# Replacing a list planner by a written-out time for every piece of work

## The chip, the cores and the metric

The kernel runs on one core of one Trainium2 chip. A core has five engines with a queue of instructions each: TensorE (PE), VectorE (DVE), ScalarE (ACT), GpSimd (POOL) and SyncE (SP). Each works through its own list in order, and a semaphore holds an instruction until work of another engine is done. The time is device microseconds (us) of one launch; lower is better.

## The reference, cut to what matters

`x` is 2048 tokens by 512. Four layers follow one another, A, B, A, B, each added to `x` after a layer norm.

```
# A: attention over segments of 32 tokens, 8 memory rows carried from segment to segment
mem = mem0
for s in range(64):
    h = concatenate([mem, x[32*s : 32*s+32]])            # 40 rows
    q, k, v = h@Wq, h@Wk, h@Wv                           # 32 heads of 128
    p = softmax(mask(q @ k.T * scale))                   # mask: the memory columns are open
    o = (p @ v) @ Wo
    mem = o[:8];  outs.append(o[8:])                     # the next segment needs mem

# B: linear attention, 32 heads of 16
q, k, v = split(x @ wqkv);  phi = where(t > 0, t+1, exp(t)) + 1e-6
kv = phi(k).T @ v;  z = sum(phi(k))                      # over all 2048 tokens
o = (phi(q) @ kv) / (phi(q) @ z) @ wo
```

So an A layer is a recurrence of 64 steps that can't be split: the memory rows of step s+1 come out of the whole of step s. A B layer needs sums over all tokens before its second half can begin.

## The kernel before, in words

All weights lie in SBUF. `a_layer` is called twice, and each call walks 64 steps; four steps make a tile of 128 tokens. A step consists of these pieces (names as in the code, with the profile's lines):

- `k0`, `k1`, `q0`, `q1`, `v0`, `v1`: `project`, six PSUM tiles of four nodes each. A node is four matmuls side by side, each on 32 columns of the array, 512 wide (L811 for q and k, L815 for v). Each tile is copied to SBUF by ACT or DVE (L625 or L626; `evac` lets the planner choose), and for q and k DVE turns it with a STREAM_TRANSPOSE (L834).
- `mem0`, `mem1`: attention of the 8 memory rows, for two halves of the heads: scores (L916, L910), exp on ACT (L927), two products on DVE (L937), sums on PE (L751), log and exp on ACT (L947, L949), values on PE (L751), a product on DVE (L960).
- `out`: eight nodes of eight 256-wide matmuls (L1056), the first four reading the first half of the heads, then two copies into `outW_sb`.
- `next`: two small PE nodes (L1081) and one copy, which give the memory rows of the next step. The chain k, q, mem, out, next is the recurrence.
- `x`: attention of the 32 token rows, whose result is only needed by the `out` of the following step (L978, L992, L988, L995, L997, L999, L1000, four copies `Pbx` of 32x256, L1011, PE L751).
- `res`: rows of the result go through `y_sb` (L1092) and by small DMAs of POOL (L641) into `dx_sb`, and are added to `x`.

Every fourth step has more: `prep` (layer norm of the next tile and its transposition, L776), `left0`, `left1`, `leftv0`, `leftv1`, `lefts` (q, k, v of the last 8 rows of the tile's four segments, six tiles more of `project`), the rows of `out` that belong to them (`left_rows`), `bi` (`b_in`: first half of B for a finished tile), and in the second A layer `bo` (`b_out`: second half of B for a tile of the layer before).

Nothing is emitted in the order of the code. `_Prog.add` records a node with its reads, writes and PSUM tiles; `_Prog.schedule` is a list planner. It keeps a clock for every engine, gives each node a duration from formulas (`c_act`, `c_dve`, `c_pe4`), and hands each engine the ready node of highest priority:

```
nd.prio = -(step * PERIOD + OFFSET[name][k])             # PERIOD = 13.5, OFFSET a table of 600 numbers by name
spare = 0 if tiles[oldest[0]] in nd.tiles else 1 if nd.urgent else 2
if bf is None or bf[1] > tn + EPS or n_free(tn + EPS) <= spare:
    kept.append(item)                                    # no PSUM bank for it: wait
```

A first writer of a PSUM tile takes one of eight banks, and a tile that is not `urgent` (not on the recurrence) has to leave two banks free and to wait until all other inputs of its later nodes are done (`soft`). All nodes of one tile are chained in the order of the code: each waits for the one before.

Two helpers add matmuls that compute nothing that is used: `warm` (14 of 512 in the first step, L742) and `keep_busy` (151 of 256, L1352), the latter around the ends of both A layers.

`_Prog.finalize` turns dependences into semaphore waits, and `emit` writes each engine's list.

## Time and profile before

| | |
|---|---|
| median of 3 runs | 1823.23 us (1821.59 to 1824.45) |
| profiled execution: its own time | 1821.27 us |
| profiled execution: span from first to last instruction | 1819.1 us, mean granted clock 0.995 |
| PE busy | 1626.0 us, 89% of the span, 53422 matmuls |
| DVE busy | 1175.7 us, 65% |
| ACT busy | 1137.4 us, 63% |
| POOL busy | 327.1 us, 18% |

A matmul's recorded duration holds its way through the array, so PE can be counted busy while no matmul is being fed. "Idle before" a group is time in which the engine stood still just before one of its instructions, with the work that ended the wait behind the arrow. `PEclk` is the share of full speed that PE's clock was granted. The chain that ended last is followed back from the last instruction.

In the trace the first layer A runs from the first `k` of step 1 at 53.48 us to the `out` of step 64 (the token rows of the last segment) at 878.92 us, the second from 925.48 us to 1780.00 us.

### The profile page before, as it was taken

The numbers are of one execution on the slowest core, as the hardware profiler recorded it, in microseconds if no ns is written. First come the engines' busy times: TensorE is split into PE (matmuls) and PEld (weight loads), VectorE is DVE, ScalarE is ACT, GpSimd is POOL, SyncE is SP. The second block draws the span as 40 slices with busy tenths as digits, with TensorE's granted clock in tenths as the row PEclk, the third lists the DMA queues.
The fourth block names the chain that finished last, engine by engine and source line by source line (L and its number), as shares of the span: only waits on it lengthen the run. The fifth ranks groups of instructions, "written<-read, shape, count | busy, mean of one in ns | idle before, by whom it ended". The sixth has DMA issues, their size and how long they took to land.

```text
span 1819.1 us, 115216 instructions
## 1 busy us (share of the span) xinstructions
PE 1626.0 (89%) x53422; PEld 1044.7 (57%) x53422; DVE 1175.7 (65%) x3945; ACT 1137.4 (63%) x3132; POOL 327.1 (18%) x660
## 2 busy tenths in 40 slices
PE   5899888999998999899989989999889999889898
PEld 2556555655555565555655555555555565555564
DVE  3566666666666666666566766666666666666667
ACT  3566666666666666666466666666666666666655
POOL 2012121111212111112101221121211121211121
PEclk9999999999999999999999999999999999999999
DMA  9100000000000000000000000000000000000004
GB/s 377 54 15 13 16 16 12 12 15 16 13 15 16 12 13 15 16 15 19 16 8 12 19 15 16 18 18 12 18 15 15 18 16 15 18 13 17 24 13 142
DMA packets 34929, 51.66 MB, mean 28 GB/s; under 512 B 13432, under 2 KB 28592, under 8 KB 32912
## 3 DMA queue, kind: packets, MB, share of 16 engines
q0 software_dynamic: 21744, 19.78, 3.8%
q1 hardware_dynamic: 11120, 11.94, 2.0%
q10 hardware_dynamic: 1584, 12.58, 1.7%
q8 instruction: 417, 6.83, 1.5%
q14 instruction: 64, 0.52, 0.1%
HBM read 29.63 MB, written 10.49 MB: 22 GB/s over the span
## 4 chain that ended last, share of the span: by engine, by line
PE 72%; DVE 12%; ACT 10%; DMA 3%; issue 3%; POOL 0%; DVEq 0%; ACTq 0%
PE pb L811 31%; PE pb L815 13%; PE pb L1056 12%; PE pb L751 10%; DVE arena_sb L626 5%; ACT arena_sb L625 4%; DVE arena_sb L960 2%; ACT outW_sb L625 2%; PE pb L910 2%; DMA Wk_sb<-in_A_Wk_dram 1%; DVE arena_sb L999 1%; PE pb L776 1%; ACT arena_sb L949 1%; PE pb L1081 1%; ACT arena_sb L927 1%
## 5 line engine op out<-in xcount | busy, mean ns | idle before, releaser
L625 ACT ACTIVATE arena_sb<-pb 128x512 bf16<-128x512 f32 (+6 forms) x1423 | 696.5, 502 | 357.9 <-PE pb L811 198.7
L834 DVE STREAM_TRANSPOSE arena_sb<-arena_sb 128x256 f32<-128x256 f32 x640 | 278.7, 440 | 269.7 <-ACT arena_sb L625 268.7
L641 POOL DMA_DIRECT2D dx_sb<-y_sb x504 | 254.4, 511 | 1056.6 <-DVE y_sb L1092 565.9
L1056 PE MATMUL pb<-Wo_sb,arena_sb 128*32 128x256 bf16 x10368 | 349.3, 274 | 58.9 <-DVE arena_sb L960 55.2
L751 PE MATMUL pb<-arena_sb 128*32 128x128 bf16 (+2 forms) x14320 | 333.2, 223 | 46.5 <-DVE arena_sb L626 23.8
L811 PE MATMUL pb<-Wk_sb,arena_sb 128*32 128x512 bf16 x5120 | 337.6, 383 | 37.9 <-ACT arena_sb L625 16.5
L815 PE MATMUL pb<-Wv_sb,arena_sb 128*32 128x512 bf16 x5120 | 348.3, 378 | 0.5 <-issue 0.4
L811 PE MATMUL pb<-Wq_sb,arena_sb 128*32 128x512 bf16 x5120 | 341.9, 382 | 0.7 <-DMA Wq_sb<-in_A_Wq_dram 0.6
L1056 PEld LDWEIGHTS pb<-Wo_sb,arena_sb 128*32 128x32 bf16 x10368 | 256.2, 97 | 107.1 <-DVE arena_sb L960 81.5
L751 PEld LDWEIGHTS pb<-arena_sb 128*32 128x32 bf16 x14320 | 232.5, 96 | 137.0 <-DVE arena_sb L626 47.8
L626 DVE CAST arena_sb<-pb 128x128 bf16<-128x128 f32 (+3 forms) x351 | 162.7, 470 | 104.0 <-PE pb L815 55.1
L811 PEld LDWEIGHTS pb<-Wk_sb,arena_sb 128*32 128x32 bf16 x5120 | 127.2, 97 | 159.1 <-ACT arena_sb L625 27.2
L811 PEld LDWEIGHTS pb<-Wq_sb,arena_sb 128*32 128x32 bf16 x5120 | 137.1, 97 | 125.0 <-issue 4.0
L625 ACT ACTIVATE outW_sb<-pb 128x128 fp32r<-128x128 f32 x247 | 68.5, 277 | 161.8 <-PE pb L1056 154.1
L626 DVE COPY arena_sb<-arena_sb 32x256 bf16<-32x256 bf16 (+1 forms) x615 | 130.9, 213 | 46.1 <-PE pb L910 26.2
L815 PEld LDWEIGHTS pb<-Wv_sb,arena_sb 128*32 128x32 bf16 x5120 | 123.9, 95 | 64.0 <-issue 2.1
L927 ACT ACTIVATE arena_sb<-pb 128x192 bf16<-128x192 f32 (+1 forms) x256 | 84.1, 328 | 59.5 <-PE pb L910 57.5
L960 DVE TENSOR_TENSOR arena_sb<-pb,arena_sb 128x128 bf16<-128x128 f32 x252 | 71.7, 287 | 70.0 <-PE pb L751 37.9
L937 DVE TENSOR_TENSOR arena_sb<-arena_sb 128x128 bf16<-128x128 bf16 x504 | 88.5, 216 | 9.2 <-ACT arena_sb L927 7.2
L1092 DVE TENSOR_TENSOR y_sb<-pb,outW_sb 64x256 bf16<-64x256 f32 x158 | 65.8, 416 | 27.1 <-ACT outW_sb L625 23.5
L751 PE MATMUL pb<-arena_sb,one_sb 128*32 128x128 bf16 x2016 | 71.9, 220 | 10.1 <-DVE arena_sb L937 10.1
L751 PEld LDWEIGHTS pb<-arena_sb,one_sb 128*32 128x32 bf16 x2016 | 48.8, 96 | 47.8 <-DVE arena_sb L937 27.6
(103 smaller groups left out, 1524.1 us busy)
## 6 DMA issues: line engine op xcount, KB each, us to landing
Wq_sb<-in_A_Wq_dram ACTq DMA_DIRECT2D x1, 4096.0 KB, 13.8
Wk_sb<-in_A_Wk_dram ACTq DMA_DIRECT2D x1, 4096.0 KB, 24.5
Wv_sb<-in_A_Wv_dram ACTq DMA_DIRECT2D x1, 4096.0 KB, 34.9
Wo_sb<-in_A_Wo_dram SPq DMA_DIRECT2D x4, 1024.0 KB, 11.8
xs_scratch<-x_sb POOLq DMA_DIRECT2D x32, 128.0 KB, 2.3
pq_scratch<-arena_sb POOLq DMA_DIRECT2D x32, 128.0 KB, 2.0
dx_sb<-y_sb POOLq DMA_DIRECT2D x252, 12.0 KB, 1.7
dx_sb<-y_sb POOLq DMA_DIRECT2D x252, 4.0 KB, 1.8
```

What stands on the lines that cost most here:

```text
L625: return e.activation(o() if callable(o) else o, i() if callable(i) else i, ACTF.Copy)
L626: return e.tensor_copy(o() if callable(o) else o, i() if callable(i) else i)
L641: add(eng, lambda e: e.dma_start(o, i), 0.55 if eng == "pool" else 0.4, reads=reads, writes=writes, dsem="%s%d" % (kind, k), lat=lat + (0. ...
L751: r = pe.matmul(o[q], w[:, q], x, start=start, stop=stop, skip_group_check=True, tile_position=(0, 32 * j))
L811: r = pe.matmul(tl.f32()[32 * j:32 * j + 32, 0:512].rearrange("p (i j f) -> p i j f", i=4, j=4), blk[:, c, :], w, start=(c == 0), stop=(c ...
L815: r = pe.matmul(tl.f32()[32 * j:32 * j + 32, 0:512], blk[:, c, :], W[:, c, o:o + 512], start=(c == 0), stop=(c == 3), tile_position=(0, 32 ...
L834: add("dve", lambda v: v.transpose(dst, src(img[:, k, :].bitcast(F32))), c_dve(256), reads=[("img", k)], writes=[dkey], urgent=urgent)
L927: add("act", lambda a: a.activation(PQ[:, r2, b, 0:nq], tl.f32()[:, 0:nq], ACTF.Exp, scale=SCALE), c_act(nq), tiles=[tl], writes=[("PQ", r ...
L937: add("dve", lambda v, a=a, p_=p_, w_=w_: v.tensor_tensor(wide(Pm[:, k, a, :]), p_.unsqueeze(2).to_broadcast([128, 4, 4, 8]), w_, ALU.mult ...
L960: add("dve", lambda v: v.tensor_tensor(oTb[:, s % NO, 16 * b:16 * b + 16, 0:8], pv.f32()[:, 0:128].rearrange("p (n q) -> p n q", q=8), Rm[ ...
L1056: r = pe.matmul(tl.f32()[32 * j:32 * j + 32, 0:256], oT[:, 4 * hh + n, :], Wo_sb[:, 8 * n + hh, 256 * d:256 * d + 256], start=(hh == 0 and ...
L1092: add("dve", lambda v: v.tensor_tensor(y_sb[0:64, k, :], tl.f32()[0:64, 0:256], outW[64:128, w, :].bitcast(F32), ALU.add), c_dve(256), rea ...
```

## The change

The planner goes. Each node carries a written time, in ns, and often a letter for its engine (a for ACT, v for DVE). For each layer `PERIOD` holds a length of four steps, an offset, and a table by name and step modulo four; `OWN` has entries for single steps, mainly near both ends of each layer, which come before the table.

```
PERIOD = {
    0: (44811, 8548, {
        'k0': {
            0: '27075 27835 28266 28482 28937a 29591',
...
        'next': {
            0: '37244 37304 37674a',
            1: '48363 48423 48793a',
...
    1: (47082, 762505, {
...
OWN = {
    (0, 0, 'next'): '49733 49894 50264v',
...
def when(key, engs):
    layer, step, name, k = key
    own = _OWN.get((layer, step, name), ())
    if k < len(own) and own[k] is not None:
        t, eng = own[k]
    else:
        n, o, table = _PERIOD[layer]
        t, eng = table[name][step % 4][k]
        t += o + n * (step // 4)
    return t, eng or engs[0]
```

The times are used for one thing: the order. `schedule` becomes a sort, a walk that hands out banks (the one whose last reader stands earliest), and a pass over the readers of each tile:

```
for nd in self.nodes:
    nd.t, nd.eng = when(nd.key, nd.engs)
seq = sorted(self.nodes, key=lambda n: (n.t, n.idx))
...
        b = min(free)[1]
        if owner[b] is not None:
            for o in owner[b].ops:
                (nd.order if o.eng == "pe" and nd.eng == "pe" else nd.sync).add(o)
...
for tl in {tl for nd in seq for tl in nd.tiles}:
    ops = sorted(tl.ops, key=lambda o: place[o])
    for i, nd in enumerate(ops):
        if nd.eng != "pe":
            for o in ops[:i]:
                if o.eng not in ("pe", nd.eng):
                    nd.sync.add(o)
self.committed = seq
```

In `add` a reader of a tile now waits for the last matmul of the tile rather than for the reader that stands before it in the code; readers on different engines wait for one another in the order of their times, readers on one engine need no wait. Further:

```
-    def warm(step, n, after):
...
-    def keep_busy():
...
-    keep_busy()
+    P.before["act"] = add("act", lambda a: a.preload_act_table_set("natural_log_exp_and_others"), 1.3)
-                add("pe", mm, c_pe4(4, 512), reads=[key] + bkeys, tiles=[tl], urgent=urgent, mode="col")
+                add("pe", mm, 0.2155, reads=[key] + bkeys, tiles=[tl])
```

The last pair stands for many such edits of a node's duration. `urgent`, `soft`, the spare banks, `mode` and the fence are gone. The nodes that compute something are the same.

How the order comes out can be read without a run, from the two built programs. The four-step pattern of PE in the middle of the first layer, from the `out` of one step to the projections of the next (line numbers of the changed file: L1560 is `out`, L1584 `next`, L1318 q and k, L1322 v; in brackets what an instruction waits for):

```
L1560 Matmult pb<-Wo_sb,arena_sb 32x256 [s_act,s_dve]
L1560 Matmult pb<-Wo_sb,arena_sb 32x256 x31
L1318 Matmult pb<-Wq_sb,arena_sb 32x512 x4
L1318 Matmult pb<-Wk_sb,arena_sb 32x512 x4
L1318 Matmult pb<-Wq_sb,arena_sb 32x512 x4
L1584 Matmult pb<-selm_sb,outW_sb 32x16 [s_dve]
L1584 Matmult pb<-selm_sb,outW_sb 32x16 x3
L1322 Matmult pb<-Wv_sb,arena_sb 32x512 [s_act]
L1322 Matmult pb<-Wv_sb,arena_sb 32x512 x3
L1584 Matmult pb<-selm_sb,outW_sb 32x16 [s_act]
L1584 Matmult pb<-selm_sb,outW_sb 32x16 x3
L1318 Matmult pb<-Wq_sb,arena_sb 32x512 x4
L1318 Matmult pb<-Wk_sb,arena_sb 32x512 x4
L1318 Matmult pb<-Wq_sb,arena_sb 32x512 x4
L1318 Matmult pb<-Wk_sb,arena_sb 32x512 [s_act]
L1318 Matmult pb<-Wk_sb,arena_sb 32x512 x11
```

Before, the same place in the program reads:

```
L1056 Matmult pb<-Wo_sb,arena_sb 32x256 [s_dve]
L1056 Matmult pb<-Wo_sb,arena_sb 32x256 x31
L751 Matmult pb<-arena_sb 32x128 [s_dve]
L751 Matmult pb<-arena_sb 32x128 x11
L751 Matmult pb<-arena_sb 32x128 [s_dve]
L751 Matmult pb<-arena_sb 32x128 x3
L751 Matmult pb<-arena_sb 32x16x8 x4
L1081 Matmult pb<-selm_sb,outW_sb 32x16 [s_act]
L1081 Matmult pb<-selm_sb,outW_sb 32x16 x3
L751 Matmult pb<-arena_sb 32x128 x12
L751 Matmult pb<-arena_sb 32x128 [s_dve]
L751 Matmult pb<-arena_sb 32x128 x3
L751 Matmult pb<-arena_sb 32x16x8 x4
L1081 Matmult pb<-selm_sb,outW_sb 32x16 [s_act]
L1081 Matmult pb<-selm_sb,outW_sb 32x16 x3
L811 Matmult pb<-Wk_sb,arena_sb 32x512 [s_dve]
L811 Matmult pb<-Wk_sb,arena_sb 32x512 x19
```

Counted over the whole program: 165 matmuls fewer on PE (the helpers'); matmuls that carry a wait 2140 before and 2483 after, waits that stand alone on PE 56 and 322. Of the copies, 158 of 32x256 and 54 of 128x128 in SBUF go from DVE to ACT, 43 of the `outW_sb` copies too; 102 of 128x512 out of PSUM and 37 of 128x384 go from ACT to DVE. SP's eight loads of the last stage, four before of one array and then four of the other, are mixed (two, one, two, three).

## The prediction

> **What bounds the kernel now.** I read the page first: busy shares, the clock, the chain that ended last; then PE's waits; then PE's timeline over four steps.

> ```profile
> PE 1626.0 (89%) x53422; PEld 1044.7 (57%) x53422; DVE 1175.7 (65%) x3945; ACT 1137.4 (63%) x3132; POOL 327.1 (18%) x660
> PEclk9999999999999999999999999999999999999999
> PE 72%; DVE 12%; ACT 10%; DMA 3%; issue 3%; POOL 0%; DVEq 0%; ACTq 0%
> ```

> PE leads, at full clock, yet 22% of the chain lies on DVE and ACT: PE isn't saturated, it stands in a ring with them. Whom it waits for (total, times, longest):

> ```profile
> PE pb L1056 <- DVE arena_sb L960: 55.2, 104, 1.0
> PE pb L751 <- DVE arena_sb L626: 23.8, 60, 2.6
> PE pb L811 <- ACT arena_sb L625: 16.5, 46, 0.6
> PE pb L811 <- DVE arena_sb L626: 15.8, 39, 0.7
> PE pb L751 <- issue: 4.0, 6, 1.7
> ```

> All are links of the recurrence: `out` waits for the memory product, the next projections for the copy after `next`. In one step of the timeline (start, duration, idle before):

> ```profile
> 656.97 1.26 PE L811 MATMUL pb<-Wk_sb,arena_sb 128*32 128x512 bf16 x20 [0.34 <-DVE arena_sb L626]
> 658.06 1.04 PE L811 MATMUL pb<-Wq_sb,arena_sb 128*32 128x512 bf16 x16
> 658.92 0.82 PE L811 MATMUL pb<-Wk_sb,arena_sb 128*32 128x512 bf16 x12
> ...
> 662.30 0.39 PE L815 MATMUL pb<-Wv_sb,arena_sb 128*32 128x512 bf16 x4
> 663.07 0.29 PE L751 MATMUL pb<-arena_sb,one_sb 128*32 128x128 bf16 x8 [0.38 <-DVE arena_sb L937]
> ...
> 664.55 1.93 PE L1056 MATMUL pb<-Wo_sb,arena_sb 128*32 128x256 bf16 x64 [0.40 <-DVE arena_sb L960]
> 666.70 0.46 PE L751 MATMUL pb<-arena_sb 128*32 128x128 bf16 x20 [0.22 <-DVE arena_sb L626]
> ...
> 667.92 1.26 PE L811 MATMUL pb<-Wk_sb,arena_sb 128*32 128x512 bf16 x20 [0.37 <-DVE arena_sb L626]
> ```

> Two things are to be seen. Where work is at hand PE is fed without a hole: 16 matmuls in 658.92-658.06=0.86 us, 53.9 ns each. And each step has five holes; a hole is longer than "idle before" says, since the last matmul's way through the array (1.93 us for 64, of which 64x27.2 ns=1.74 is feeding) counts as busy.

> **What PE must do.** Feeding times by such differences: 53.9 ns (512 wide), 27.2 (256), 13.9 (128), some 7 (32 to 64). In four steps: 480 of k, q, v, left and 32 of `b_in` at 512 wide, 27.6 us; 320 of `out`, 8.7; 368 at 128 wide, 5.1; 16 of L992, 0.4; some 400 small ones, 2.8. Sum **44.6 us, 11.15 a step**. `b_out` adds 16 at 512 and 16 at 128 in layer two: 45.7, 11.43 a step. Before takes (878.92-53.48)/63=13.10 and (1780.00-925.48)/63=13.56. So 1.95 and 2.13 us a step are holes: 123+134=257 us. More can't be won in the steps.

> **The change part by part.**

> *The order.* I compare PE work standing between a producer and its consumer in the new order (front part, and the same period's other rows) with the traced chain between them.
> - `out` to `next`: drain 0.17, copy into `outW_sb` 0.28, two hand-overs of 0.03 to 0.05: 0.52 us. New cover: 12 matmuls of 512, 0.65; in the other three step kinds 0.65 to 0.79. Before: 0.22 idle here after 0.2 of drain.
> - `next` to k: drain 0.17, copy 0.20, hand-overs 0.08: 0.45. Cover 0.58 to 0.65, by `left` and values of the token rows. Before: 0.34 to 0.39 idle.
> - Scores to sums: drain 0.17, exp 0.33, two products 0.36, hand-overs 0.12: 0.98. Cover: 16 of L1322, 24 of 128 wide, the other half's scores: 1.3. Before: 0.38 idle.
> - Sums to `out`: drain 0.17, L947 0.28, L949 0.31, L960 0.29, hand-overs 0.15: 1.20. Cover 1.5 to 1.7. Before: 0.40.

> Every hole has cover, by 0.1 to 0.5 us. The cover holds only if ACT or DVE isn't busy with something else when its turn comes. *Engine letters*: ACT gains 158x411 (32x256 copies) +54x309+43x277 and loses 102x597+37x489 ns, with small ones +19 us; DVE loses 158x219+54x192+43x289 and gains 102x689+37x554, +29 us. That is 1156 and 1205 us, 73% and 76% of some 1590: both below PE (1471 us of feeding, 92%), but fuller than now, so queues form. From none to half of the holes can stay. I take 0.28 us a step: 0.08 is the trace's own `issue` pauses (some 10 us, no order removes them), 0.20 about one thin cover missed per step. Nearest row: from 688.31 to 707.62 us, where `left` gave PE enough to do, the timeline shows no idle at all; that speaks for the low end.

> *Waits on PE*: 266 more that stand alone. Nearest row: L992, which waits for ACT and DVE, starts at 701.53, just 8x53.9 ns after 701.10 when L815 began. Price 0; upper end 0.05 each, 13 us. *Readers in time order, no waits between readers on one engine, banks by earliest release*: these are in the order; alone they could cost a bank wait or save one hand-over (0.05 us) per tile; 0, both ends inside the holes above. *Durations in `add`*: nothing reads them now; 0. *POOL's and SP's order*: row DMAs land in 1.7 to 1.8 us and are needed many us later except at the ends; the last stage's eight loads still start together after step 63's `out`; 0, -2 to +3.

> *The helpers.* They fed PE 151x107 ns+3.0=19 us, in holes of the layer ends; on the path they cost next to nothing (at 895.24 they end 0.17 after the work they delay), so removal gains under 1 us. What they bought is the clock:

> ```profile
> 24.00:27.00 3.00, 1.23 (x12) 0.46 (x16) 0.00 (x0) 0.00 (x0) 0.00 (x0) 0.50 1.03 429
> 894.00:897.00 3.00, 3.00 (x36) 1.97 (x34) 1.39 (x3) 0.35 (x1) 0.54 (x1) 1.00 0.23 76
> 912.00:915.00 3.00, 1.71 (x92) 1.03 (x92) 2.80 (x12) 2.89 (x9) 0.00 (x0) 0.92 0.15 44
> 915.00:918.00 3.00, 2.78 (x68) 1.63 (x68) 2.67 (x12) 2.19 (x10) 0.00 (x0) 0.51 0.00 0
> ```

> (stretch, length, PE busy, then the other engines; third from the end PEclk.) With helpers the serial part at 894 keeps 1.00; after PE's pause at 21.2 to 25.8, and again after a half-idle stretch at 912, it is halved for some 3 us. [...]

> **The sum**, on the profiled execution's span: head to step 1, 52.5 (53.48 before; bound by the weight DMAs, the last q/k/v one landing after 34.9). Layer one 63x(11.15+0.28)=720. Between the layers, 46.6 before: the serial chain from `out` at 878.92 to the first `left` at 899.85 stays, 20.9; +3 for the clock; then step 0, 25.6 before with a DMA wait of 2.76 on its chain, now some 15 (its PE work is near 14): 39. Layer two 63x(11.43+0.28)=738. Tail, 39.1 before: ACT's Ln and Exp of 16 tiles bound it in any order; less 1 for order, +3 for the clock: 41. Sum 1590.5. The profiled run is 2.2 longer than its span, and the median 2.0 above it: **1595 us**, 12.5% less.

> **The rivals.**
> 1. *The plan holds to the letter*: no hole stays, PE feeds always. 1595-126x0.28=1560. For: every cover is positive. Against: margins of 0.1 us with ACT and DVE at 75%. 15%.
> 2. *Half the holes return as queueing on ACT and DVE*, whose order can't adapt: 1.0 us a step instead of 0.28 is +92: 1687. For: 32x256 copies of 0.41 on ACT may stand ahead of the copy on the chain. Against: the dense stretch above. 20%.
> 3. *Slower*: head-of-line blocking. In the new list a 32x256 copy that waits for DVE (L999 of the token rows) stands ahead of ACT's copies of q and k; if the token chain (exp, sums, log, exp, two products) is late by d, the recurrence is late by d in every step. It decides from d=2.1 us a step beyond its cover (228/126=1.81 on top of the 0.28): all that the order wins. The token chain's pieces sum to some 3 us and it has most of a step. 4%.
> 4. *Nothing changes*: the recurrence's latency, not idle order, sets 13 us. Against: its pieces (k and q 3.5, drain to scores 1.9, mem 2.7, `out` 1.8, `next` 1.5) give 11.4 even in a row, and halves overlap. 1%.

> My forecast, between 1 and 2, 60%. The range 1555 to 1668 takes 1, the clock's and waits' upper ends and some of 2. Faster by over 0.2% (about what a measurement of this kernel can tell) 95%, within it 1%, slower 4%.

> **What would show it.** Right: `out <- L960`, `L811 <- copies` each under a third of now; k to k some 11.4 and 11.7 us; PE busy near all of each mid-kernel slice; DVE and ACT at 73 to 76%; PEclk of 0.5 to 0.8 at the layers' ends and nowhere else. Wrong: PE waits on ACT's copies of q and k of half a us each (case 2), or POOL's row DMAs on the chain in mid-layer, or a lower clock in the steps.

## The result, and the profile after

The kernel with the written order takes **1699.62 us** (median of 4, 1698.46 to 1702.65) against 1823.84 for the kernel before, measured beside it (4 runs, 1821.59 to 1824.46): a ratio of **0.9324, 95% interval 0.9307 to 0.934**. It is faster, as forecast, but 105 us slower than the forecast 1595, and 32 us outside the range. The profiled execution took 1702.65 us, its span 1700.9.

From the profile, in the same order as before the change (busy shares, PE's clock, the chain that ended last):

```profile
PE 1555.4 (91%) x53257; PEld 1096.2 (64%) x53257; DVE 1170.0 (69%) x3811; ACT 1133.5 (67%) x3266; POOL 325.7 (19%) x660
PEclk9999999999999999999899999999999999999998
PE 82%; DVE 6%; issue 6%; ACT 4%; DMA 2%; POOL 0%; DVEq 0%; ACTq 0%
```

DVE's and ACT's share of the chain fell from 22% to 10%. But `issue` doubled from 3% to 6%: time in which PE waited for nothing that the profile shows. PE's waits (total us, times, longest):

```profile
PE pb L1560 <- issue: 26.0, 35, 3.8
PE pb L1261 <- issue: 25.0, 36, 1.4
PE pb L1318 <- DMA Wq_sb<-in_A_Wq_dram: 20.1, 1, 20.1
...
PE pb L1318 <- ACT arena_sb L1150: 5.2, 16, 0.4
...
PE pb L1560 <- DVE arena_sb L1466: 0.2, 1, 0.2
```

L1560 is `out`, L1466 the memory product ahead of it: 55.2 us of waiting became 0.2. So the order did what it was to do. In its place stand `issue`, some 70 us over all lines (about 10 before), and one wait of 20 us for Wq at the start.

By stage, with the same marks as in the prediction:

| stage | forecast | after | excess |
|---|---|---|---|
| head, to the first projection of step 1 | 52.5 | 61.08 | 8.6 |
| layer one, 63 steps | 11.43 each | (827.46-61.08)/63=12.17 | 0.74 each, 46 |
| between the layers | 39 | 867.29-827.46=39.8 | 0.8 |
| layer two, 63 steps | 11.71 each | (1657.32-867.29)/63=12.54 | 0.83 each, 52 |
| tail | 41 | 43.6 | 2.6 |

The sum of the excess is the 110 us by which the span missed 1590.5. Nine tenths of it lie in the steps. PE's timeline in one step shows what kind of pause it is (start, duration, form, number of matmuls, idle before):

```profile
640.95 1.55 PE L1560 MATMUL pb<-Wo_sb,arena_sb 128*32 128x256 bf16 x48
643.23 0.40 PE L1560 MATMUL pb<-Wo_sb,arena_sb 128*32 128x256 bf16 x6 [0.73 <-issue]
643.36 0.89 PE L1261 MATMUL pb<-arena_sb 128*32 128x128 bf16 x46
644.03 0.21 PE L1584 MATMUL pb<-selm_sb,outW_sb 128*32 128x16 f32 x4
644.08 0.23 PE L1261 MATMUL pb<-arena_sb 128*32 128x128 bf16 x2
644.13 0.29 PE L1584 MATMUL pb<-selm_sb,outW_sb 128*32 128x16 f32 x12
644.25 0.29 PE L1498 MATMUL pb<-arena_sb,bo_sb 128*32 128x256 bf16 x4
644.36 0.21 PE L1494 MATMUL pb<-arena_sb,bo_sb 128*32 128x64 bf16 x4
644.39 0.63 PE L1261 MATMUL pb<-arena_sb 128*32 128x128 bf16 x32
644.84 0.83 PE L1318 MATMUL pb<-Wk_sb,arena_sb 128*32 128x512 bf16 x12
645.48 0.40 PE L1318 MATMUL pb<-Wq_sb,arena_sb 128*32 128x512 bf16 x4
645.70 0.39 PE L1318 MATMUL pb<-Wk_sb,arena_sb 128*32 128x512 bf16 x2
646.98 0.39 PE L1318 MATMUL pb<-Wk_sb,arena_sb 128*32 128x512 bf16 x2 [0.90 <-issue]
```

Both pauses stand in the middle of a node: after 58 of the 64 matmuls of `out`, and after two of a node's four. No semaphore is waited for there. From one pause to the next there are 6+46+4+2+12+4+4+32+12+4+2=**128 matmuls**. With a weight load each that is 256 instructions. The DMA table has a queue that carries PE's instructions (packets, MB, share of the 16 engines):

```profile
q8 instruction: 417, 6.83, 1.7%
```

6.83 MB in 417 packets is 16,384 bytes each, and PE's 2x53257 instructions and 322 stand-alone waits, divided by 256, make 417.3; out512 (below), with 5184 matmuls and as many weight loads fewer, has 377 packets in this queue. I call the 256 instructions of such a packet a page. The 128 matmuls above were fed in 645.70+2x0.054-643.23=2.58 us, and the next page was there 3.75 us after the first.

Setting the trace's packets of q8 beside PE's starts (worked out from the trace): 194 of the 417 pages begin with a pause, 115 us in all (start to start of the two matmuls, less 40 ns). The pause stands ahead of instruction 192 of each 256 (within 2), counted from PE's first. So do all 107 of the profile's `issue` waits of PE (70.5 us), and all 16 (10.3 us) of the kernel before. PE resumes 1.26 to 1.56 us after a packet's end (10th to 90th percentile). In the median a packet starts 1.1 us after PE enters a page and takes 1.03 us; a page that ends in a pause has then lasted 3.5 us. 99 of 100 packets start at least 3.3 us after the one before. At 416 of the 417 places where PE enters a page, the packets that had ended were just as many as the pages entered before it. So here only one page was fetched ahead, and over several pages PE got no more than 128 matmuls in some 3.3 to 3.5 us (a single page can be shorter, down to 2.4 us, where the one before it was long). In the two layers the pauses come to 0.90 and 0.86 us a step. By the same count the kernel before has 36 of them, 18 us.

### The profile page after: what moved, and what is told of

Same layout as the page of the kernel before. It is cut to its first block, busy times and chain, and to the rows that moved or that the text cites. A ratio compares the mean times of both kernels' runs of the same rounds, so it can differ in the third digit from the quotient of the medians.

```text
span 1700.9 us, 115242 instructions
## 1 busy us (share of the span) xinstructions
PE 1555.4 (91%) x53257; PEld 1096.2 (64%) x53257; DVE 1170.0 (69%) x3811; ACT 1133.5 (67%) x3266; POOL 325.7 (19%) x660
## 3 DMA queue, kind: packets, MB, share of 16 engines
q8 instruction: 417, 6.83, 1.7%
## 4 chain that ended last, share of the span: by engine, by line
PE 82%; DVE 6%; issue 6%; ACT 4%; DMA 2%; POOL 0%; DVEq 0%; ACTq 0%
PE pb L1318 30%; PE pb L1560 18%; PE pb L1261 14%; PE pb L1322 14%; ACT arena_sb L1150 2%; DMA Wq_sb<-in_A_Wq_dram 2%; PE pb L1417 2%; PE pb L1584 1%; DVE arena_sb L1151 1%; PE pb L1286 1%; DVE st_sb L1272 1%; DVE arena_sb L1444 1%; PE pb L1498 1%; DVE arena_sb L1341 1%; DVE Wq_sb L1829 0%
## 5 line engine op out<-in xcount | busy, mean ns | idle before, releaser
L1150 ACT ACTIVATE arena_sb<-pb 128x512 bf16<-128x512 f32 (+4 forms) x1303 | 603.5, 488 | 309.6 <-PE pb L1318 190.7
L1261 PE MATMUL pb<-arena_sb 128*32 128x128 bf16 (+2 forms) x14320 | 429.0, 224 | 28.6 <-issue 21.4
L1318 PE MATMUL pb<-Wk_sb,arena_sb 128*32 128x512 bf16 x5120 | 437.3, 381 | 9.0 <-ACT arena_sb L1150 5.2
L1318 PE MATMUL pb<-Wq_sb,arena_sb 128*32 128x512 bf16 x5120 | 424.3, 380 | 22.3 <-DMA Wq_sb<-in_A_Wq_dram 20.1
L1322 PE MATMUL pb<-Wv_sb,arena_sb 128*32 128x512 bf16 x5120 | 415.2, 378 | 2.4 <-issue 1.7
L1560 PE MATMUL pb<-Wo_sb,arena_sb 128*32 128x256 bf16 x10368 | 372.0, 273 | 29.2 <-issue 26.0
L1261 PEld LDWEIGHTS pb<-arena_sb 128*32 128x32 bf16 x14320 | 283.8, 96 | 100.5 <-issue 34.2
L1560 PEld LDWEIGHTS pb<-Wo_sb,arena_sb 128*32 128x32 bf16 x10368 | 269.7, 96 | 75.3 <-issue 41.8
L1151 DVE CAST arena_sb<-pb 128x512 bf16<-128x512 f32 (+3 forms) x440 | 230.4, 527 | 103.7 <-PE pb L1318 64.2
L1318 PEld LDWEIGHTS pb<-Wq_sb,arena_sb 128*32 128x32 bf16 x5120 | 163.1, 97 | 109.8 <-DMA Wq_sb<-in_A_Wq_dram 20.3
L1318 PEld LDWEIGHTS pb<-Wk_sb,arena_sb 128*32 128x32 bf16 x5120 | 164.5, 97 | 103.3 <-issue 11.8
L1322 PEld LDWEIGHTS pb<-Wv_sb,arena_sb 128*32 128x32 bf16 x5120 | 143.9, 95 | 49.1 <-issue 4.3
L1150 ACT ACTIVATE arena_sb<-arena_sb 32x256 bf16<-32x256 bf16 (+1 forms) x365 | 132.5, 363 | 13.4 <-DVE arena_sb L1505 8.2
L1466 DVE TENSOR_TENSOR arena_sb<-pb,arena_sb 128x128 bf16<-128x128 f32 x252 | 73.1, 291 | 71.5 <-PE pb L1261 48.0
L1151 DVE COPY arena_sb<-arena_sb 32x256 bf16<-32x256 bf16 (+1 forms) x403 | 82.0, 209 | 8.2
L1455 ACT ACTIVATE arena_sb<-arena_sb 128x128 f32<-128x128 f32 x252 | 78.1, 310 | 5.9
## 6 DMA issues: line engine op xcount, KB each, us to landing
Wv_sb<-in_A_Wv_dram ACTq DMA_DIRECT2D x1, 4096.0 KB, 13.7
Wk_sb<-in_A_Wk_dram ACTq DMA_DIRECT2D x1, 4096.0 KB, 23.1
Wq_sb<-in_A_Wq_dram ACTq DMA_DIRECT2D x1, 4096.0 KB, 33.5
```

Source lines behind the costliest of these rows:

```text
L1150: return e.activation(o() if callable(o) else o, i() if callable(i) else i, ACTF.Copy)
L1151: return e.tensor_copy(o() if callable(o) else o, i() if callable(i) else i)
L1261: r = pe.matmul(o[q], w[:, q], x, start=start, stop=stop, skip_group_check=True, tile_position=(0, 32 * j))
L1318: r = pe.matmul(tl.f32()[32 * j:32 * j + 32, 0:512].rearrange("p (i j f) -> p i j f", i=4, j=4), blk[:, c, :], w, start=(c == 0), stop=(c ...
L1322: r = pe.matmul(tl.f32()[32 * j:32 * j + 32, 0:512], blk[:, c, :], W[:, c, o:o + 512], start=(c == 0), stop=(c == 3), tile_position=(0, 32 ...
L1455: add("act", lambda a: a.activation(Rm[:, k, :], Rm[:, k, :], ACTF.Exp, scale=-1.0), c_act(128, 0, 1), reads=[("Rm", k)], writes=[("Rm", k)])
```

## The experiments

**Theory 1**: the supply of PE's instructions, one page per 3.3 to 3.5 us, stops PE wherever 128 successive matmuls are narrow, and the holes of the kernel before gave it the time. **Theory 2**: the 266 more stand-alone waits on PE make the pauses. **Theory 3**: the rows' DMA traffic slows the supply. **Rival 2 of the prediction**: queueing on ACT and DVE. For theory 1 I sum over all pages of a program what the feeding lacks to 3.3 us: 121 us for this kernel. That sum is an estimate "on paper"; the pauses counted in a trace are the measurement. The runs were made in three groups on three chips, and a kernel's time differs by up to 20 us between them (below), so each run is set against one measured beside it where there is one.

**out512: fewer instructions, the same feeding.**

```
-for i in range(2):
-    for j in range(4):                      # n = 2*(j//2) + i, d = j % 2
-        pe.matmul(tl[32*j.., 0:256], oT[:, 4*hh+n, :], Wo_sb[:, 8*n+hh, 256*d:256*d+256], ...)
+for j in range(4):
+    pe.matmul(tl[32*j.., 0:512], oT[:, 4*hh+j, :], Wo_sb[:, 8*j+hh, 0:512], ...)
```

> The changed kernel, with `out_proj` issuing 32 matmuls of 512 columns for its 64 of 256 (the same feeding: 32x53.9=1.72 us against 64x27.2=1.74; the copies behind it read the first 256 columns only, so the output is left incomplete: the sum over two of the four row groups and half the columns are left out). It takes away 5184 matmuls and as many weight loads, 40 pages, and nothing from the feeding or from any wait. Theory 1 (page supply): what is missing to 3.3 us a page falls from 121 to 61 us, so about 60 us less: 1640 (1630 to 1655). Theory 2 (stand-alone waits) and theory 3 (DMA traffic of the rows slows the supply): 1700, within 5.

1640.43 us (1637.80 to 1642.52), ratio to the kernel before 0.8968 (0.8949 to 0.8986). Its busy times:

```profile
PE 1533.9 (94%) x48073; PEld 962.7 (59%) x48073; DVE 1169.1 (71%) x3811; ACT 1134.8 (69%) x3266; POOL 327.0 (20%) x660
```

As theory 1 has it. No wait and no feeding went, 5184 matmuls did; the pauses at page ends fell to 52 us, PE's share rose to 94%. Theories 2 and 3 expected no change. That the time fell just on the 1640 expected is in part luck: the expectation starts from 1700, and the changed kernel was not measured beside this run. wq_first (below) was: 1711.67 us, with a head 9.9 us shorter and some 133 us of pauses. Set against that, the edit won 81 us of time and as much in pauses.

**before_out512: the same edit in the kernel before.**

> The kernel before the change, its order kept, with `out_proj` issuing 32 matmuls of 512 columns for its 64 of 256 (as in the run out512; half of the result is left out in the same way). It takes 40.5 pages from the stream, and on paper as much of what is missing to 3.3 us a page: 115 to 43 us. Theory 1: the holes in which PE waits for DVE and ACT have been giving the supply time, and only some 18 us of pauses stand at page ends in its trace; so 5 to 20 us less than the kernel before, against 60 in the changed kernel. Rival (matmuls of 512 columns are simply cheaper than two of 256): 60 us less here too.

1811.04 us (1809.40 to 1812.87) beside 1823.28, ratio 0.9933 (0.9916 to 0.995): 12 us. So 512-wide matmuls are not cheaper as such. On paper the kernel before lacks as much in its pages (115 us), but its holes covered that; its pauses at page ends went from 18 to 12 us.

**shift: the same program, moved by half a page.**

```
 for nd in by[eng]:
+    if eng == "pe" and nd is first:         # the first projection
+        for _ in range(256):                # two waits to an instruction
+            e.wait_ge(self.sems["pool"], 1)
```

> The changed kernel with 128 more instructions at one place only: semaphore waits that are long satisfied, ahead of PE's first projection, where PE waits some 20 us for Wq anyhow. They move the rest of PE's stream by half a page of 256. In the two profiles of the changed kernel the pauses stand ahead of instruction 192 of every 256 counted from PE's start, whatever that instruction is. Theory 1 (page supply): counted in the program as it was, the pauses now stand ahead of instruction 64 of every 256, so at other matmuls than before; some 180 to 210 of them, and the time within 15 us of 1700. Theory 2 (something in the nodes themselves, a wait or the kind of matmul): the pauses stay at the same matmuls.

1701.82 us, one run. 188 pauses, 112 us. The stretch of the timeline above, in this run (line numbers 4 higher; L1588 is `next`, L1322 `project` for q and k):

```profile
637.12 0.29 PE L1588 MATMUL pb<-selm_sb,outW_sb 128*32 128x16 f32 x10
638.30 0.22 PE L1588 MATMUL pb<-selm_sb,outW_sb 128*32 128x16 f32 x3 [0.89 <-issue]
...
639.77 0.44 PE L1322 MATMUL pb<-Wk_sb,arena_sb 128*32 128x512 bf16 x4
```

The pause ahead of the six matmuls of `out` is gone, and one stands 64 matmuls later (6+46+4+2+6), after the tenth of `next`; Wk's node of four runs through. Over the whole program: where the repeated run of the changed kernel (below) pauses, its starts lie 634 ns apart in the mean; at the same matmuls this run has 48 ns, and none of the two kernels' 184 and 188 pauses fall on the same matmul. So the pauses belong to the place in the page, not to any node or wait. That rules theory 2 out as the main cause.

**more_waits: twice the stand-alone waits.**

```
 for nd in by[eng]:
+    if eng == "pe" and len(nd.waits) > 1:
+        for _ in range(2):
+            e.wait_ge(self.sems[self.names[nd.waits[0][0]]], nd.waits[0][1])
```

> The changed kernel with one more stand-alone semaphore wait on PE, already satisfied, ahead of each PE instruction group that has more than one wait: 641 stand-alone waits instead of 322. Theory 2 (each stand-alone wait stops PE; 322 of them make the pauses of some 110 us, 0.3 us each): up to 100 us more, 1800. Theory 1 (a wait is only one more instruction of a page): 319 instructions are 1.2 pages, so 1 to 5 us more: 1701 to 1705.

1743.37 us (1742.64 to 1746.66), on a chip where the kernel before took 1828.58. The changed kernel was not measured beside it; wq_first was, at 1711.67, and its head is 9.9 us shorter, so the addition costs 1743.4-1711.7-9.9=22 us. Both theories missed: far from 100, but more than 5. Matmul by matmul against wq_first: at the 420 places that newly have such a wait the starts lie 17.2 us further apart in sum, **41 ns each in the mean**; a stand-alone wait isn't free. The pauses at page ends grew by 17 us more, and all other spacings gave 8 us back. Why 319 instructions, 1.2 pages, lengthen the pauses by so much was not followed up.

**merged: a quarter of the instructions of `tiled`.**

```
-for j in range(4):
-    q = slice(32 * j, 32 * j + 32)
-    r = pe.matmul(o[q], w[:, q], x, ..., tile_position=(0, 32 * j))
+return pe.matmul(o, w[:, 0:128], x, ...)
```

> The changed kernel, with the helper `tiled` written as one matmul with a 128-column stationary instead of four with 32 columns each on the four column tiles: the same products, 12,996 fewer matmuls and as many fewer weight loads (102 pages of 256 instructions of the 417), the feeding time equal by the widths (4x13.9 ns against 128 columns once). Theory 1 (a page of 256 PE instructions cannot be had faster than one in some 3.3 us, so pages full of narrow matmuls make PE wait): summed over the program's pages, what is missing to 3.3 us falls from 121 us to 3 us, so about 1585 to 1600 if changing between tiled and whole matmuls is free. Theory 2 (the stand-alone semaphore waits on PE cost the pauses): none of them is taken away, 1700. A cost of changing between the two ways of using the array, which no run has shown so far, would show as new pauses at each change and could make it slower than 1700; then the pauses at the page ends must still be gone.

1798.27 us (1794.74 to 1799.27), ratio to the kernel before 0.9827 (0.9805 to 0.9849): nearly all that the change had won is gone. Two pauses at page ends are left in the whole run, 1.6 us: what theory 1 said of the supply holds. The time went elsewhere. PE's timeline (L1319 is `project`, L1259 the merged matmul):

```profile
648.32 0.39 PE L1319 MATMUL pb<-Wv_sb,arena_sb 128*32 128x512 bf16 x4
648.64 0.23 PE L1259 MATMUL pb<-arena_sb 128*128 128x128 bf16 x1
648.80 0.40 PE L1319 MATMUL pb<-Wv_sb,arena_sb 128*32 128x512 bf16 x4
```

Four matmuls of 53.9 ns end feeding at 648.54; the whole one starts at 648.64. It is fed by 648.69 (128 columns at four times 13.9 ns), and the next starts at 648.80. So each change between 32-column and whole use costs 0.10 to 0.11 us here. Over the whole run it is alike: from the last 512-wide matmul of a node to a whole one the starts lie 312 ns apart in the median (570 times), to other 32-column work 206; from a whole one of 128 columns back to a 512-wide node 149 ns (543 times), to the next whole one 56. The program has 2140 changes, 214 us. With wq_first beside it: 1711.7+9.9, less its 133 us of pauses, plus 2 and 214, makes 1805.

**no_ln: less work on ACT.**

```
-add("act", ... activation(Rx, tl[:, 0:256], ACTF.Ln), ...)
-add("act", ... activation(Rx, Rx, ACTF.Exp, scale=-1.0), ...)
+P.count += 1
+add("act", ... activation(Rx, tl[:, 0:256], ACTF.Exp, scale=-0.01), ...)
```

> The changed kernel without ACT's logarithm in the normalization of the token rows (the exponential reads the sums directly, so the weights of the token rows are left unnormalized). It takes one operation of 0.38 us a step off ACT and off the token chain: 64x0.38=24 us of ACT's work in each layer's steps, 48 in all. Rival from the prediction (the holes returned as queueing on ACT and DVE): 20 to 48 us less, since what stands in ACT's queue behind it comes earlier. Theory 1 (page supply): no PE instruction goes, so 1700 within 6 on a chip like the first.

1692.70 us (1687.92 to 1696.95), ratio to the kernel before 0.9288 (0.9258 to 0.9318); the changed kernel has 0.9315 (0.9286 to 0.9344) in the run below, on another chip. Some 5 us, which the intervals don't tell from nothing, for 48 us of ACT's work: queueing on ACT isn't what the steps hang on.

**wq_first: the loads in the old order, and the changed kernel again.**

```
-(0, -9, 'setup'): '1039 1139 2994 2940 1039 26839 ...
+(0, -9, 'setup'): '1039 1139 1040 1041 1042 26839 ...
```

> The changed kernel, with the times of the three weight loads on ACT's queue set so that they go out as Wq, Wk, Wv (as before the change) instead of Wv, Wk, Wq. Theory of the head: the first projections need Wq, which now lands last at 33.5 us; with Wq first PE's 20.07 us wait at 15.3 goes, the first projections of step 1 come at about 53.5 instead of 61.1, and the kernel takes 7 to 8 us less: about 1692. Rival (the head is bound by the number of weight bytes or by the first token chain, not by their order): within 2 us of 1699.6.

1711.67 us (1707.17 to 1716.89): a miss, 20 us above the expectation. The first `next` came at 50.49 us instead of 60.34, as expected, but each step took 0.15 us more than in the changed kernel. On that chip the kernel before took 1828.58, and a page's packet 1.10 us instead of 1.02. So both were run once more, side by side on another chip.

> The changed kernel itself once more, as the partner of the runs beside it. In the run with the loads reordered the median transfer of a page of PE instructions took 1.10 us where the changed kernel's first profile has 1.02. If the steps hang on the page supply (theory 1), 80 ns more a page are worth, from the sum over the pages (121 us missing at 3.3 us a page, 141 at 3.4), some 17 us, so this kernel is at 1700 on a chip whose transfers take 1.02 us and at some 1715 where they take 1.10. If the reordered loads themselves slowed the steps, it stays at 1700 whatever the transfers take.

> The kernel with Wq, Wk, Wv loaded in this order, beside the changed kernel on one chip. Theory of the head: 9 to 11 us less than that kernel (its head was 9.85 us shorter), with the same time a step. Rival (the order of the loads does something to the steps): the same or slower than it, 0.15 us a step more.

again: 1697.89 us (1692.89 to 1704.89), packets 0.99 us. wq_first_b: 1690.93 us (1689.72 to 1691.50), packets 1.02 us; the first `next` at 50.18 instead of 59.85, and 0.04 us a step more than again. The order of the loads is worth 7 us, a little under the 9 to 11 expected. PE's wait for weights in wq_first_b:

```profile
PE pb L1318 <- DMA Wk_sb<-in_A_Wk_dram: 7.0, 1, 7.0
```

7 us instead of 20: Wq is used while Wk still comes. The same kernel took 1711.67 and 1690.93 us on two chips, and its two traces have some 133 and 113 us of pauses at page ends: the 20 us lie there. That agrees with theory 1, where 80 ns more a page are worth some 17 us, but the packets' time was not varied by itself.

**wq_pvm: whole matmuls in one place only.** wq_first, and in `pvm` five matmuls of 128 columns for twenty of 32 (`whole` is `tiled` as in merged):

```
-tiled(pe, pv[:, 0:128], vleft[:, g2, b, g, :], Pm[:, k, 1, :], True, False)
+whole(pe, pv[:, 0:128], vleft[:, g2, b, g, :], Pm[:, k, 1, :], True, False)
...
-    r = tiled(pe, pv[:, o], vimg[:, r2, 128 * hh:128 * hh + 128], Pm[:, k, 0, o], False, i == 3)
+    r = whole(pe, pv[:, o], vimg[:, r2, 128 * hh:128 * hh + 128], Pm[:, k, 0, o], False, i == 3)
```

> The kernel with the loads reordered, and the products of the values for the memory rows (`pvm`, 20 of `tiled`'s matmuls a half step) as 5 whole-array matmuls: 3780 matmuls fewer, 29.5 pages fewer. Theory 1 (page supply) with a change between tiled and whole taken at 0.10 us from the run where all of `tiled` was merged: what is missing to 3.3 us a page falls from 121 to 48 us, the 504 changes more cost 50: some 22 us less than with the loads reordered alone (10 to 30). Rival (the changes stand in the chain from the memory product to `out` and are paid twice): the same or slower.

**1639.04 us** (1635.31 to 1642.44), ratio to the kernel before 0.8989 (0.8969 to 0.9009): 52 us less than wq_first_b, more than the 10 to 30 expected, and the fastest kernel here that computes all of the reference.

```profile
PE 1569.0 (96%) x49477; PEld 1052.9 (64%) x49477; DVE 1168.7 (71%) x3811; ACT 1143.0 (70%) x3266; POOL 325.8 (20%) x660
```

Of PE's waits the largest `issue` row is now

```profile
PE pb L1264 <- issue: 6.4, 9, 3.0
```

where the changed kernel has 26.0 and 25.0. The pauses at page ends went from 112 to 24 us, 88 rather than the 73 summed. And the changes cost less in net, since five whole matmuls are fed faster than twenty tiled ones, which I had left out:

```profile
645.96 0.39 PE L1325 MATMUL pb<-Wv_sb,arena_sb 128*32 128x512 bf16 x4
646.28 0.32 PE L1258 MATMUL pb<-arena_sb 128*128 128x128 bf16 x5
646.53 0.29 PE L1264 MATMUL pb<-arena_sb 128*32 128x128 bf16 x8
```

From the end of feeding at 645.96+0.216=646.18 to 646.53 it is 0.35 us with both changes; twenty tiled ones took 703.46-703.28=0.18 in the kernel before. 0.17 net, 252 times, is 43 us; 88-43=45 of the 52, and 7 us stay unexplained.

Theory 3 was not tried by taking the rows' DMAs away. out512 leaves them as they are, and its pauses fell with the pages. The changed kernel's trace speaks against the theory too: of the instruction packets between 65 and 1640 us, 262 met no other DMA packet and took 1.08 us in the mean; the third of all that met the most took 1.11. In the tail there is one place that looks like it:

```profile
1662.04 2.09 PE L1560 MATMUL pb<-Wo_sb,arena_sb 128*32 128x256 bf16 x36 [3.77 <-issue]
```

Here SP's eight loads of 0.4 to 0.5 MB are under way (the DMA engines' busy share was 0.97 from 1657 to 1660 and 1.07 from 1660 to 1663); the page's packet started at 1659.80, 5.4 us after PE had entered the page before (1654.41), instead of 1.1. That pause recurs (3.2 us in again, 3.0 in wq_first_b and wq_pvm). That the loads delay the packet is argued from the order of events, not shown.

## Why the prediction was wrong, by its own steps

- **What PE must do** held: the steps have the same matmuls as before, so 11.15 and 11.43 us a step of feeding are still in them. "Where work is at hand PE is fed without a hole" did not. It was read from matmuls of 512 columns, of which a page lasts 128x53.9 ns=6.9 us. By the same estimate a page of 256-column ones lasts 128x27.2 ns=3.48 us, at the 3.3 to 3.5 measured; of 128-column ones 128x13.9 ns=1.8, far below them.
- **The step that failed** is the hole that stays: 0.28 us a step. Measured: 1.02 and 1.11. Of that, 0.90 and 0.86 are pauses at page ends, which the prediction had at 0.08, "the trace's own `issue` pauses (some 10 us, no order removes them)". That no order removes them was not shown, but an order can call them forth: 18 us of pauses at page ends before, 115 after. They were small before because PE's holes let the supply catch up (115 us lacked there on paper, too). The terms that I got right in kind, the missed covers, leave 0.12 and 0.25 for 0.20. A step that fills holes was costed as if nothing stood right behind the holes. The trace of the kernel before had the sign in two places that the prediction read past. It called `PE pb L751 <- issue` a link of the recurrence, which it isn't: nothing is waited for there. And the dense stretch that it took as its nearest row, up to 707.62 us, runs straight into a pause in the middle of a run of like matmuls:

```profile
707.62 0.84 PE L751 MATMUL pb<-arena_sb 128*32 128x128 bf16 x46
709.81 0.23 PE L751 MATMUL pb<-arena_sb 128*32 128x128 bf16 x2 [1.35 <-issue]
```

That pause stands at a page end too, and ends 1.45 us after a packet. So this row spoke for a limit of dense work, not for the low end.
- **The order** did hold: `out` behind the memory product and the projections behind the copies wait for under a third of before (0.2 for 55.2 us; 5.2 for 16.5). ACT's and DVE's work did not grow by the 19 and 29 us of the sum over the engine letters: it came to 1133 and 1170 us, a little below the kernel before, where 1156 and 1205 were forecast. Why was not followed up.
- **Waits on PE**, price 0, upper end 0.05 us each: 41 ns each by more_waits, so 266 more cost, by estimate, some 11 us, inside the 0.12 and 0.25 above.
- **POOL's and SP's order**: 0 for the head missed a queue that the prediction did not look at. On ACT's queue the new times send Wv, Wk, Wq, and Wq, needed first, lands last (33.5 us after its issue, Wv 13.7, Wk 23.1): 8.6 us, of which wq_first_b gave back 7 in the median.
- **The helpers and the clock**: the 3 us a layer end that the sum has for the clock are a term that no run shows. What the runs showed in its place: between the layers the serial part, 850.56-827.46=23.1 us from `out` to the next projections, was 2.2 us longer than the 20.9 of the kernel before; with the 16.7 after it, for 15, it was 39.8 us for 39. PE was at half clock there as expected (third from the end is PEclk):

```profile
834.00:837.00 3.00, 2.68 (x40) 1.34 (x44) 0.96 (x3) 0.60 (x1) 0.54 (x1) 0.50 0.15 49
```

  The forecast had this at the layers' ends and nowhere else. PE was fed at near half speed in the head too, though `PEclk` reads 1.00 there: after the wait for Wq, 60 matmuls of 512 took 41.27-35.35=5.92 us, 99 ns each instead of 53.9. The kernel before has such a stretch as well (64 of them in some 6 us from 14.70), so it does not explain the miss.
- **The tail** was 43.6 for 41, with the pause of 3.77 us in it, and with PEclk at 0.50 from 1665 to 1671.
- **Rival 2** has the number that came nearest, 1687, by the wrong mechanism; that is luck. PE's waits for ACT and DVE in the steps stayed small, and no_ln shows that ACT's queue isn't the limit; DVE's was not varied, and only the small waits (3.2 us at most in one row, apart from the layer norm at the layers' ends) speak against it. Rivals 1, 3 and 4 fell.

## What to carry to other kernels

Before pricing the filling of holes, ask what was hidden in them. For PE count instructions, not only feeding: in these runs a page was 128 matmuls with their weight loads and came every 3.3 to 3.5 us, so by estimate stretches that averaged under 3.3/128, some 26 ns a matmul, waited for instructions, and pauses that repeated every 128 matmuls in the middle of a node, with `issue` as the releaser, were the sign of it. Fewer, wider matmuls with the same feeding then gave time (out512, 81 us); where that meant changing between tiled and whole use of the array, each change cost 0.10 to 0.11 us (merged), and the instructions saved between two changes must be worth more than that.
